# Pattern shifts as 64-bit additions on GpSimd, and two head groups' rows merged by DMA before one normalisation

## The chip, the cores and the metric

The kernel runs on one core of a Trainium2 chip. The core has five engines that run side by side: TensorE (PE in the profile, its weight loads PEld), ScalarE (ACT), VectorE (DVE), GpSimd (POOL) and SyncE (SP), which here issues the DMAs. The metric is the time of one execution on the device in microseconds (us). The kernel before took 688.67 us, the median of three runs (687.15 to 691.1).

## The reference

`x` is 2048 tokens by 512 features. Attention has 32 heads of 16 features, and a gated feed-forward part of width 1792 stands beside it; both read the same normalised input.

```
xn  = layernorm(x)
q, k, v = (xn @ wqkv), 32 heads of 16
p   = softmax(q k^T / 4)                  # 32 x 2048 x 2048 numbers
att = (p v) @ wo
g   = xn @ W_gate ;  u = xn @ W_up
glu = (max(g, 0) * u) @ W_down
out = x + att + glu
```

The softmax needs 32 x 2048 x 2048 exponentials, and most of the kernel is arranged around them.

## The kernel before

**Tiling.** Queries are cut into 4 blocks of 512 (`c4`), heads into 4 groups of 8 (`gg`), each group into two sub-groups of 4 heads (`ee`), and keys into 16 tiles of 128 (`kt`). That makes 32 blocks (c4, gg, ee) of 16 key tiles, 512 pieces in all. For one piece TensorE forms the scores of 4 heads, 128 keys by 512 queries each; something takes their exponential; and TensorE multiplies the result by the values `v_aug`. Beside the 16 values of a head `v_aug` has columns of ones, so the same product also gives the softmax's sum, in a row of its own. All these matmuls are 64 x 32 tiles of the PE array, so eight of them run side by side: two halves of the rows (`half`) by four column strips.

**Two ways to an exponential.** Most pieces go to ScalarE: two "units" each, one ACTIVATE Exp of 128 x 1024 (L1506) that reads two PSUM banks (L1504 writes them; there are two such pairs, `P_sc`) and writes one of 16 slots of `ring`. 153 pieces, called VectorE groups or quads here (`quad`, L1451), are approximated instead. VectorE adds a bias to the scores and rounds to 16-bit integers, whose bits read as bf16 give 2 to that power with a straight-line fraction (L1459, four per group, PSUM to `qd`). Two more patterns of the same 2048 numbers follow, with 31 and 81 added to every integer; the value product uses all three, which averages the error away. So a VectorE group costs TensorE three value products where a ScalarE piece costs one. `QUADS` lists how many groups each of the 32 blocks has, 359 pieces are left to ScalarE, and that makes 718 exponential instructions.

**Where the two patterns are made.** A shift is an integer addition on 128 x 2048 16-bit numbers. On GpSimd it is done as 32-bit additions of 31 x 65537 or 81 x 65537, in two pieces of 128 x 512 words (L1475, `POOL_PIECES`), with the constant broadcast from the tensor `shift` (L704). On VectorE it is one 16-bit tensor_scalar (L1479). `POOL_SHARE` and `POOL1_SHARE` say which share goes to GpSimd: all of the second patterns and 0.6 of the first. Those of the last two groups (`LASTD`) stay on VectorE.

**Normalisation** (`normalise`, L1326 on). When a block's value product is complete, VectorE copies it from PSUM to one of two `o_sb` buffers (L1338). A DMA gathers the sums (`rsum`, L1354), VectorE takes reciprocals (L1355), a DMA puts them on the rows of `rb` (L1358), VectorE spreads them over 16 rows each (STREAM_SHUFFLE, L1365), and GpSimd multiplies (L1369 for ee = 0, L1374 for ee = 1). The values of ee = 0 stand in rows 0 to 15 of each strip of 32 and those of ee = 1 in rows 16 to 31, so GpSimd adds the two products (L1377) to one `oT` tile for the output projection. This is done for 31 blocks; the last has a chain of its own (`normalise_last`).

**Order.** Nothing is ordered by the chip. `Graph.run` places every operation in time with durations written into the code (904 ns for the exponential, 601 for L1459, `POOL_NS` for a pattern and so on), some slack after DMAs (`REC_SLACK`, `MUL_SLACK`) and a priority for each engine; each engine's program is then that fixed order, with semaphore waits between engines. Background work for TensorE (projections of q, k and v, the feed-forward part, the output projection) is spread as jobs over the units. `JOB_SHIFT` and `QUAD_SHIFT` move 15 jobs by some units and 22 groups by one key tile.

Of the kernel before, what the change touches and what calls it, by code (L numbers as in the profile page):

```python
# [5 lines left out]
BF16 = mybir.dt.bfloat16  # L6
FP32 = mybir.dt.float32
I32 = mybir.dt.int32
I16 = mybir.dt.int16
U16 = mybir.dt.uint16  # L10
ACTF = mybir.ActivationFunctionType
ALU = mybir.AluOpType
# [4 lines left out]
DH = 16  # L17
# [4 lines left out]
NB = 4  # L22
NGG = 4
# [42 lines left out]
EV_DVE = ()  # L66
XN_WAIT = 0
SPREAD_NS = 660
ADD_NS = 1100
# [3 lines left out]
QUAD_SHIFT = {(4, 4): -1, (30, 1): 1, (26, 0): -1, (20, 2): -1, (30, 2): 1, (27, 0): 1, (7, 0): 1, (6, 0): -1, (4, 3): 1, (18, 2): -1, (9, 3): 1, (11, 1): -1, (11, 0): 1, (8, 1): -1, (29, 1): -1, (6, 1): 1, (30, 4): -1, (31, 3): -1, (27, 2): -1, (20, 4): -1, (21, 3): 1, (21, 0): 1}  # L73
XN_POOL = ()
XN_NS = 2080
RBZ_AT = 20
# [1 line left out]
P1_OFF = 0  # L78
# [10 lines left out]
SHIFTS = (0, 31, 81)  # L89
# [514 lines left out]
def bass_parallel_sum__mha_block__glu_gated_reglu__prompt_kernel(  # L604
# [13 lines left out]
    with ExitStack() as es:  # L618
        def sb(name, shape, dt):
            return es.enter_context(nc.sbuf_tensor(name, shape, dt))  # L620

        ident = sb("ident", [128, 128], BF16)
        ints = sb("ints", [128, 4], I32)
        pid, shift = ints[:, 0:2], ints[:, 2:4]
# [29 lines left out]
        rsum = sb("rsum", [128, 2, 16], FP32)  # L654
        rrec = sb("rrec", [128, 2, 16], FP32)
        oT1 = sb("oT1", [128, 2, 512], BF16)
# [5 lines left out]
        G = Graph()  # L662
# [11 lines left out]
        P_o = Pool("o", 2)  # L674
        P_rb = Pool("rb", 2)
        P_oT = Pool("oT", 8)
        P_o1 = Pool("o1", 2)
        P_xr = Pool("xr", 2)


# [21 lines left out]
        t_vones, t_woz, t_selp, t_shift = Tile(), Tile(), Tile(), Tile()  # L702
        for i in range(2):
            G.op("POOL", 200, lambda e, i=i: e.iota(shift[:, i:i + 1], pattern=[[0, 1]], base=SHIFTS[i + 1] * 65537, channel_multiplier=0), writes=[t_shift], prio=14, after=14)  # L704
        G.op("POOL", 300, lambda e: e.tensor_copy(identf[:], ident[:]), reads=[t_id], writes=[t_selp], prio=15, after=25)
        G.op("POOL", 100, lambda e: e.tensor_copy(selp[:], ident[:, DH - 1:128:32]), reads=[t_id], writes=[t_selp], prio=16, after=26)
        G.op("POOL", 2500, lambda e: e.memset(v_aug[:, :, :, DH:VW], 1.0), writes=[t_vones], prio=-500)
# [75 lines left out]
        def ln_block(b, pr):  # L783
# [7 lines left out]
            def inv(m, n, rd, wr):  # L791
                t_ve = Tile()
                G.op("DVE" if single else "POOL", 66 if single else 230, lambda e: e.tensor_scalar(vare[:, m:m + n], mv[:, m:m + n, 1], EPS, None, op0=ALU.add),
                     reads=[rd], writes=[t_ve], prio=pr)
                G.op("POOL", 400 + 160 * n, lambda e: e.tensor_tensor(rstd[:, m:m + n], vare[:, m:m + n], expo[:, 0:n], ALU.pow),  # L795
                     reads=[t_ve, t_expo], writes=[wr], prio=pr)
            for i in range(4):
                m = 4 * b + i
                t_st, t_mv = Tile(), Tile()
# [31 lines left out]
            for i in range(4):  # L831
# [43 lines left out]
                elif half == 1:  # L875
# [203 lines left out]
        for b in range(1, NB):  # L1079
            ln_block(b, LN_AT[b])  # L1080
            proj_k(0, b, LN_AT[b] + 1, gap=0.02)
        for kt in range(NT):
            proj_v(kt, V_AT[kt // 4] + 2 * (kt % 4), allowed=(1, 2, 3))

# [10 lines left out]
        def oT_of(t):  # L1095
            return x_sb[:, t.slot, :]
# [136 lines left out]
        busy = {int(p) for _, s, _ in plan for p in s}  # L1233


        pv_tile, last_rec, where, first_part = {}, {}, {}, {}

        def normalise_last(tp, tp_hi):

# [88 lines left out]
        def normalise(c4, gg, ee, second):  # L1328
            tp, tp_hi = pv_tile[(c4, gg, ee, second)]
            if (c4, gg, ee) == (NB - 1, NGG - 1, 1):  # L1330
                last_pv.extend(pv_tile[(c4, gg, ee, second)])
                return
            g = 2 * gg + ee
            n = c4 * 8 + g
            to = first_part.get(n)
            if to is None:
                to = Tile("o", P_o)
                G.op("DVE", 603, lambda e: e.tensor_copy(o_sb[:, to.slot, :], ps[:, BANK[tp.slot], :]), reads=[tp], writes=[to], prio=-950, name="oev%d" % n)  # L1338
                if not second:
                    first_part[n] = to  # L1340
                    return
            else:
                G.op("DVE", 603, lambda e: e.tensor_tensor(o_sb[:, to.slot, :], ps[:, BANK[tp.slot], :], o_sb[:, to.slot, :], ALU.add),
                     reads=[tp, to], joins=[to], prio=-950, name="oev%d" % n)
            if tp_hi is not tp:
                G.op("DVE", 603, lambda e: e.tensor_tensor(o_sb[:, to.slot, :], ps[:, BANK[tp_hi.slot], :], o_sb[:, to.slot, :], ALU.add),
                     reads=[tp_hi, to], joins=[to], prio=-950, name="oev%d" % n)
            pr = at_unit[place[(c4, gg, ee, NT - 1)] + 2] + 1
            ts, trr, trb = Tile("rs"), Tile("rr"), Tile("rb", P_rb, [ee])
            par = n % 2  # L1350
            if n >= 2:
                ts.r.extend(last_rec[n - 2][0].r)
                trr.r.extend(last_rec[n - 2][1].r)
            dma(lambda e: e.dma_start(rsum[:, par, :], o_sb[DH - ee:128:32, to.slot, :]), 8, reads=[to], writes=[ts], prio=pr - 50, stream=("n1", n % 4))  # L1354
            G.op("DVE", 190, lambda e: e.reciprocal(rrec[:, par, :], rsum[:, par, :]), reads=[ts], writes=[trr], prio=-940, name="rec", slack=REC_SLACK)  # L1355

            r0 = DH * ee
            dma(lambda e: e.dma_start(rb[r0:128:32, trb.slot, :], rrec[:, par, :]), 8, reads=[trr, t_rbz], writes=[trb], prio=pr - 50, stream=("n2", n % 4))  # L1358
            last_rec[n] = (ts, trr)
            if n >= len(blocks) - 3:  # L1360

                for o in ts.w + trb.w:
                    o.urgent = 1
# [3 lines left out]
            if not ee:  # L1367
                tn = t_oT[(c4, gg)] = Tile("oT", P_oT)
                G.op("POOL", 1390, lambda e: e.tensor_tensor(oT_of(tn), o_sb[:, to.slot, :], rb[:, trb.slot, :], ALU.mult),  # L1369
                     reads=[to, trb, tsp], writes=[tn], prio=pr, port=True, slack=MUL_SLACK)  # L1370
                return

            t1, tn = Tile("o1", P_o1), t_oT[(c4, gg)]
            G.op("POOL", 1390, lambda e: e.tensor_tensor(oT1[:, t1.slot, :], o_sb[:, to.slot, :], rb[:, trb.slot, :], ALU.mult),  # L1374
                 reads=[to, trb, tsp], writes=[t1], prio=pr, port=True, slack=MUL_SLACK)

            G.op("POOL", ADD_NS, lambda e: e.tensor_tensor(oT_of(tn), oT_of(tn), oT1[:, t1.slot, :], ALU.add), reads=[t1, tn], writes=[Tile()], prio=pr, port=True)  # L1377
            tn.w.append(G.ops[-1])

        pv_left, pv_ops, last_pv = {}, {}, []  # L1380
        v_flat = v_aug[:].rearrange("p kt h d -> p kt (h d)")
# [69 lines left out]
        def quad(key, u, prev):  # L1451
# [16 lines left out]
            tb, xb = made("qb")  # L1468
            nq[0] += 1
            for n, (t, x) in enumerate(((ta, xa), (tb, xb))):  # L1470
                share, off = ((POOL1_SHARE, P1_OFF), (POOL_SHARE, 0.0))[n] if nq[0] <= len(kinds) - LASTD else (0.0, 0.0)
                if int(nq[0] * share + off) > int((nq[0] - 1) * share + off):
                    m = 1024 // POOL_PIECES
                    for i in range(POOL_PIECES):
                        G.op("POOL", POOL_NS / POOL_PIECES + 60, lambda e, x=x, n=n, c=slice(i * m, i * m + m): e.tensor_tensor(  # L1475
                            x().bitcast(I32)[:, c], raw().bitcast(I32)[:, c], shift[:, n:n + 1].to_broadcast([128, m]), ALU.add),
                            reads=[ti, tq, t_shift], writes=[t] if i == 0 else [], joins=[] if i == 0 else [t], prio=u, name="p3", port=True)
                    continue
                G.op("DVE", 600, lambda e, n=n, x=x: e.tensor_scalar(x(), raw(), float(SHIFTS[n + 1]), None, op0=ALU.add),  # L1479
                     reads=[ti, tq], writes=[t], prio=u, name="d%d" % (n + 2), port=True)  # L1480
# [78 lines left out]
```

## Time and profile before

| what | before |
|---|---|
| median of three runs | 688.67 us |
| the profiled execution's span | 686.2 us |
| TensorE busy | 674.6 us, 22242 matmuls |
| ScalarE busy | 669.2 us, of it 661.4 us in 718 exponentials |
| VectorE busy | 610.8 us |
| GpSimd busy | 552.0 us, of it 485.3 us in 482 pattern pieces |
| first exponential starts, last starts | 10.4 us, 675.5 us |

The span is the profiled execution's own time, from its first instruction to its last; the page has no time around it. It is 2.5 us below the median of the runs. A row of the page's part 5 gives the line, the engine, the operation, what it writes and reads, how often it ran, then its busy time in us, the mean time of one in ns, and the engine's idle time before such instructions with what ended it. Instructions overlap at their ends, so busy time divided by the count is shorter than the mean of one.

### The profile page before, as it was taken

How to read it: one execution, taken by the hardware profiler on the slowest of the kernel's cores; microseconds unless marked ns; L12 is line 12 of the kernel's file. 1: busy time of each engine (PE TensorE's matmuls, PEld its weight loads, DVE VectorE, ACT ScalarE, POOL GpSimd, SP SyncE). 2: the span in 40 equal slices, each digit the busy share in tenths (PEclk: the TensorE clock that was granted, in tenths of full speed). 3: DMA queues.
4: the chain of work that ended last, by engine and by line, in shares of the span. 5: the costliest groups of instructions: out<-in, count | busy, mean ns of one | idle time of the engine just before them, and what ended most of it. 6: DMA issues, size and time to landing. Idle time of an engine off the chain costs nothing.

```text
span 686.2 us, 46500 instructions
## 1 busy us (share of the span) xinstructions
PE 674.6 (98%) x22242; PEld 387.1 (56%) x21226; DVE 610.8 (89%) x1059; ACT 669.2 (98%) x735; POOL 552.0 (80%) x560
## 2 busy tenths in 40 slices
PE   8999999999999999999999999999999999999997
PEld 3556655565565656665655565656455565655553
DVE  8948999999998897999999988999999888998777
ACT  7999999999999999999999999999999999999995
POOL 3522887877988989988989989899989898998780
PEclk9999999999999999999999999999999999999999
DMA  6520011132200111010100111010100121110001
GB/s 200 87 51 21 13 37 43 35 89 85 57 12 21 36 49 46 13 36 12 35 14 11 44 43 37 25 39 4 43 7 19 29 66 36 43 42 23 13 13 33
DMA packets 49561, 26.83 MB, mean 39 GB/s; under 512 B 17880, under 2 KB 49368, under 8 KB 49368
## 3 DMA queue, kind: packets, MB, share of 16 engines
q1 hardware_dynamic: 49224, 23.73, 13.3%
q8 instruction: 170, 2.79, 1.7%
q14 instruction: 23, 0.19, 0.1%
q10 hardware_dynamic: 144, 0.13, 0.1%
HBM read 18.22 MB, written 2.10 MB: 30 GB/s over the span
## 4 chain that ended last, share of the span: by engine, by line
PE 88%; ACT 8%; DVE 3%; issue 1%; DMA 0%; POOL 0%; DVEq 0%
PE ps L136 87%; ACT ring L1506 8%; DVE stats L811 1%; DVE qd L1459 0%; DMA x_sb<-in_A_x_dram 0%; DVE xn_sb L834 0%; DVE mv L813 0%; POOL rstd L795 0%; DVE xnT L879 0%; PE ps L1249 0%; DVE qT L1061 0%; DVE xn_sb L1293 0%; DVE qf L951 0%; DVE o_sb L1338 0%; DVE kT L967 0%
## 5 line engine op out<-in xcount | busy, mean ns | idle before, releaser
L1506 ACT ACTIVATE ring<-ps 128x1024 bf16<-128x1024 f32 x718 | 661.4, 1117 | 4.9 <-PE ps L136 4.1
L1475 POOL TENSOR_TENSOR qd<-qd,ints 128x512 int32<-128x512 int32 x482 | 485.3, 1040 | 94.2 <-DVE qd L1479 60.2
L136 PE MATMUL ps<-qT,kT 64*32 64x512 bf16 x8192 | 463.3, 374 | 1.8 <-ACT ring L1506 0.7
L1459 DVE TENSOR_SCALAR qd<-ps 128x512 int16<-128x512 f32 x612 | 400.8, 684 | 47.0 <-PE ps L136 42.1
L136 PE MATMUL ps<-qd,v_aug 64*32 64x512 bf16 x3672 | 297.1, 375 | 0.9 <-DVE qd L1459 0.2
L136 PE MATMUL ps<-ring,v_aug 64*32 64x512 bf16 x2872 | 251.2, 375 | 1.3 <-issue 1.0
L1439 PEld LDWEIGHTS <-kT 64*32 64x32 bf16 x8136 | 174.5, 92 | 119.7 <-issue 27.2
L1411 PEld LDWEIGHTS <-v_aug 64*32 64x32 bf16 x5584 | 135.2, 92 | 70.3 <-issue 13.3
L136 PE MATMUL ps<-xnT,wus 64*32 64x512 bf16 x1792 | 136.2, 375 | 0.0
L136 PE MATMUL ps<-xnT,wgs 64*32 64x512 bf16 x1792 | 135.6, 375 | 0.3 <-issue 0.3
L909 PEld LDWEIGHTS <-hT 64*32 64x32 bf16 x1792 | 44.4, 92 | 26.2 <-issue 4.2
L136 PE MATMUL ps<-Wd,hT 64*32 64x512 bf16 x768 | 58.2, 375 | 0.4 <-DVE qd L1459 0.4
L909 PEld LDWEIGHTS <-wgs 64*32 64x32 bf16 x1792 | 43.5, 92 | 21.8 <-issue 2.7
L909 PEld LDWEIGHTS <-wus 64*32 64x32 bf16 x1792 | 43.8, 92 | 20.1 <-issue 3.0
L1479 DVE TENSOR_SCALAR qd<-qd 128x2048 int16<-128x2048 int16 x65 | 47.9, 746 | 0.4
L1125 DVE COPY up_sb<-ps 128x512 f32<-128x512 f32 x56 | 38.5, 687 | 5.6 <-PE ps L136 5.2
L136 PE MATMUL ps<-Wk,hT 64*32 64x512 bf16 x512 | 41.7, 375 | 0.0
L136 PE MATMUL ps<-Wv,hT 64*32 64x512 bf16 x512 | 39.6, 375 | 0.3 <-issue 0.3
L1129 DVE SCALAR_TENSOR_TENSOR hT<-ps,up_sb 128x512 bf16<-128x512 f32 x56 | 38.2, 682 | 1.4 <-PE ps L136 1.4
L136 PE MATMUL ps<-Wo_p,x_sb 64*32 64x512 bf16 x480 | 37.2, 375 | 0.2
L136 PE MATMUL ps<-xnT,Wq 64*32 64x512 bf16 x480 | 35.8, 375 | 0.1
L136 PE MATMUL ps<-xnT,Wk 64*32 64x512 bf16 x480 | 35.6, 375 | 0.3 <-DVE xnT L879 0.3
(83 smaller groups left out, 307.3 us busy)
## 6 DMA issues: line engine op xcount, KB each, us to landing
wus<-in_B_W_up_dram SPq DMA_DIRECT2D x38, 128.0 KB, 2.5
wgs<-in_B_W_gate_dram SPq DMA_DIRECT2D x38, 128.0 KB, 2.4
xr_sb<-in_A_x_dram SPq DMA_DIRECT2D x16, 128.0 KB, 2.6
qT<-qf SPq DMA_DIRECT2D x120, 16.0 KB, 2.3
out_dram<-xn_sb SPq DMA_DIRECT2D x15, 128.0 KB, 1.8
x_sb<-in_A_x_dram SPq DMA_DIRECT2D x8, 128.0 KB, 2.5
Wd<-in_B_W_down_dram SPq DMA_DIRECT2D x6, 128.0 KB, 2.3
Wv<-in_A_wqkv_dram SPq DMA_DIRECT2D x1, 512.0 KB, 4.7
```

Source lines behind the costliest of these rows:

```text
L136: return e.add_instruction(mybir.InstMatmult(name=e.bass.get_next_instruction_name(), engine=mybir.EngineType.PE, ins=[e.lower_ap(x), e.lo ...
L811: G.op("DVE", 580, lambda e, m=m: e.bn_stats(stats[:, m, :], xs(m)), reads=[t_xm[m]], writes=[t_st], prio=pr, order=last_xn if m == 4 and ...
L909: e.ldweights(w()[rows, 32 * j:32 * j + 32], tile_position=(rows.start, 32 * j))
L1125: G.op("DVE", 603, lambda e: e.tensor_copy(up_sb[:, tup.slot, :], bank_of(tu)), reads=[tu], writes=[tup], prio=-590)
L1129: G.op("DVE", 603, lambda e: e.scalar_tensor_tensor(out=hT[:, th.slot, :], in0=bank_of(tg), scalar=0.0, in1=up_sb[:, tup.slot, :], op0=ALU ...
L1411: e.ldweights(vs(j), tile_position=(64 * half, 32 * j))
L1439: e.ldweights(ks(m), tile_position=(64 * half, 32 * m))
L1459: G.op("DVE", 601, lambda e, j=j, tx=tx: e.tensor_scalar(qd[:, tq.slot, 512 * j:512 * j + 512], ps[:, BANK[tx.slot], :], IBIAS[3], 0.0, op ...
L1475: G.op("POOL", POOL_NS / POOL_PIECES + 60, lambda e, x=x, n=n, c=slice(i * m, i * m + m): e.tensor_tensor(x().bitcast(I32)[:, c], raw().bi ...
L1479: G.op("DVE", 600, lambda e, n=n, x=x: e.tensor_scalar(x(), raw(), float(SHIFTS[n + 1]), None, op0=ALU.add), reads=[ti, tq], writes=[t], p ...
L1506: exp_ops[u] = G.op("ACT", 904, lambda e, tr=tr, k0=k0: e.activation(ring[:, tr.slot, :, :], ps[:, 4 * k0:4 * k0 + 2, :], ACTF.Exp, scale= ...
```

## The change

- **Patterns.** On GpSimd a pattern is one `int64_add` over 128 x 512 64-bit words (128 x 1024 32-bit words in the program) with the constant in the instruction. GpSimd makes all patterns but those of the first two groups (`FIRSTD`) and the last two (`LASTD`): 308 instructions where there were 482 pieces; VectorE makes 8 where it made 65. The operation belongs to a library that is loaded once, after the last power operation of the layernorm.
- **Normalisation.** Blocks ee = 0 and ee = 1 of a head group share it. For ee = 0 only the sums are gathered. For ee = 1 the sums are gathered too, and four DMAs of 32 KB copy rows 16 to 31 of each strip from its `o_sb` buffer into that of ee = 0. Then one reciprocal of 128 x 32, two DMAs to `rb`, one spread and one multiplication follow, the last on VectorE. The block before the last is normalised alone. So 31 reciprocals and 31 spreads become 16, and 31 multiplications and 15 additions on GpSimd become 16 multiplications on VectorE.
- **Groups.** `QUADS` has 158 groups, not 153: 354 pieces, 708 exponentials, are left to ScalarE.
- **Shifts.** `JOB_SHIFT` and `QUAD_SHIFT` are empty.

```diff
-POOL_PIECES = 2
-POOL1_SHARE = 0.6
+POOL1_SHARE = 1.0
+FIRSTD = 2
...
-JOB_SHIFT = {36: -1, 46: 6, 85: -6, 18: -2, 40: 2, 109: 4, 107: -6, 98: 4, 33: 1, 26: 6, 41: 2, 68: -1, 103: -4, 45: 1, 65: -6}
-QUAD_SHIFT = {(4, 4): -1, (30, 1): 1, (26, 0): -1, ...}
+JOB_SHIFT = {}
+QUAD_SHIFT = {}
...
-POOL_NS = 1900
-QUADS = [0, 3, 4, 5, 5, 5, 5, 5, 5, 5, 5, 5, 5, 5, 5, 5, 5, 5, 6, 5, 5, 5, 5, 5, 5, 5, 5, 5, 5, 5, 5, 5]
+POOL_NS = 1060
+LIB_NS = 7000
+LANES = 0x0001000100010001
+QUADS = [0, 3, 4, 5, 5, 6, 5, 5, 5, 5, 6, 5, 5, 5, 5, 6, 5, 5, 5, 6, 5, 5, 5, 5, 6, 5, 5, 5, 5, 6, 5, 5]
...
+        def load_library():
+            stock = [o for o in G.ops if o.eng == "POOL" and o.name == "stock"]
+            G.op("POOL", LIB_NS, lambda e: e.int64_add(word.bitcast(I64), word.bitcast(I64), 0), reads=[t_word], writes=[t_lib], prio=-790, order=stock)
...
+            if ee:
+                dma(lambda e: e.dma_start(rsum[:, par, 16:32], o_sb[DH - 1:128:32, to.slot, :]), 8, reads=[to], prio=pr - 50, stream=("n1", n % 4))
...
+                for j in range(4):
+                    rows = slice(32 * j + DH, 32 * j + 32)
+                    dma(lambda e, rows=rows: e.dma_start(o_sb[rows, toA.slot, :], o_sb[rows, to.slot, :]), 32, reads=[to], joins=[toA], prio=pr - 49, stream=("mg", j))
...
-                G.op("POOL", 1390, lambda e: e.tensor_tensor(oT_of(tn), o_sb[:, to.slot, :], rb[:, trb.slot, :], ALU.mult),
-                     reads=[to, trb, tsp], writes=[tn], prio=pr, port=True, slack=MUL_SLACK)
...
-            G.op("POOL", ADD_NS, lambda e: e.tensor_tensor(oT_of(tn), oT_of(tn), oT1[:, t1.slot, :], ALU.add), reads=[t1, tn], writes=[Tile()], prio=pr, port=True)
+            G.op("DVE", 600, lambda e: e.tensor_tensor(oT_of(tn), o_sb[:, toA.slot, :], rb[:, trb.slot, :], ALU.mult),
+                 reads=[toA, trb, tsp], writes=[tn], prio=-930, port=True, slack=MUL_SLACK, name="mul")
...
-                    for i in range(POOL_PIECES):
-                        G.op("POOL", POOL_NS / POOL_PIECES + 60, lambda e, x=x, n=n, c=slice(i * m, i * m + m): e.tensor_tensor(
-                            x().bitcast(I32)[:, c], raw().bitcast(I32)[:, c], shift[:, n:n + 1].to_broadcast([128, m]), ALU.add),
...
+                    G.op("POOL", POOL_NS, lambda e, x=x, n=n: e.int64_add(x().bitcast(I64), raw().bitcast(I64), SHIFTS[n + 1] * LANES),
+                        reads=[ti, tq, t_lib], writes=[t], prio=u, name="p3", port=True)
```

More of the change, by code (lines that the diff above doesn't have):

```diff
@@ L623, in bass_parallel_sum__mha_block__glu_gated_reglu__prompt_kernel @@
         ints = sb("ints", [128, 4], I32)
-        pid, shift = ints[:, 0:2], ints[:, 2:4]
+        pid, word = ints[:, 0:2], ints[:, 2:4]
         hmask = sb("hmask", [128, 4], FP32)
@@ L701, in bass_parallel_sum__mha_block__glu_gated_reglu__prompt_kernel @@
             t_rbz.w.append(G.ops[-1])
-        t_vones, t_woz, t_selp, t_shift = Tile(), Tile(), Tile(), Tile()
-        for i in range(2):
-            G.op("POOL", 200, lambda e, i=i: e.iota(shift[:, i:i + 1], pattern=[[0, 1]], base=SHIFTS[i + 1] * 65537, channel_multiplier=0), writes=[t_shift], prio=14, after=14)
+        t_vones, t_woz, t_selp, t_lib, t_word = Tile(), Tile(), Tile(), Tile(), Tile()
+        G.op("POOL", 100, lambda e: e.memset(word, 0), writes=[t_word], prio=-899)
         G.op("POOL", 300, lambda e: e.tensor_copy(identf[:], ident[:]), reads=[t_id], writes=[t_selp], prio=15, after=25)
@@ L1347, in normalise @@
                      reads=[tp_hi, to], joins=[to], prio=-950, name="oev%d" % n)
+            alone = (c4, gg) == (NB - 1, NGG - 1)
             pr = at_unit[place[(c4, gg, ee, NT - 1)] + 2] + 1
[L1349 to L1359, printed above, removed]
+            m = c4 * NGG + gg
+            par, r0 = m % 2, DH * ee
+            if not ee:
+                ts = Tile("rs")
+                if m >= 2:
+                    ts.r.extend(last_rec[m - 2][0].r)
+                dma(lambda e: e.dma_start(rsum[:, par, 0:16], o_sb[DH:128:32, to.slot, :]), 8, reads=[to], writes=[ts], prio=pr - 50, stream=("n1", n % 4))
+                halves[m] = to, ts, G.ops[-1]
+                if not alone:
+                    return
@@ new lines, in normalise @@
+            toA, ts, sum0 = halves[m]
+            if ee:
+                dma(lambda e: e.dma_start(rsum[:, par, 16:32], o_sb[DH - 1:128:32, to.slot, :]), 8, reads=[to], prio=pr - 50, stream=("n1", n % 4))
+                ts.w.append(G.ops[-1])
+                if m >= 2:
+                    for r in last_rec[m - 2][0].r:
+                        G.ops[-1].deps[r] = True
+                evac = [w for w in toA.w]
+                for j in range(4):
+                    rows = slice(32 * j + DH, 32 * j + 32)
+                    dma(lambda e, rows=rows: e.dma_start(o_sb[rows, toA.slot, :], o_sb[rows, to.slot, :]), 32, reads=[to], joins=[toA], prio=pr - 49, stream=("mg", j))
+                    for w in evac + [sum0]:
+                        G.ops[-1].deps[w] = True
@@ new lines, in normalise @@
+            trr, trb = Tile("rr"), Tile("rb", P_rb, [1 if alone else 0])
+            if m >= 2:
+                trr.r.extend(last_rec[m - 2][1].r)
+            w = 16 * (ee + 1)
+            G.op("DVE", 190, lambda e: e.reciprocal(rrec[:, par, 0:w], rsum[:, par, 0:w]), reads=[ts], writes=[trr], prio=-940, name="rec", slack=REC_SLACK)
+            for h in range(ee + 1):
+                dma(lambda e, h=h: e.dma_start(rb[DH * h:128:32, trb.slot, :], rrec[:, par, 16 * h:16 * h + 16]), 8, reads=[trr, t_rbz],
+                    writes=[] if h else [trb], joins=[trb] if h else [], prio=pr - 50 + 0.1 * h, stream=("n2", 2 * par + h))
+                if h:
+                    for d in G.ops[-2].deps:
+                        G.ops[-1].deps[d] = True
@@ L1360, in normalise @@
+            last_rec[m] = (ts, trr)
             if n >= len(blocks) - 3:
-                for o in ts.w + trb.w:
-                    o.urgent = 1
+                for o in ts.w + trb.w + toA.w:
+                    if o.eng == "SP":
+                        o.urgent = 1
             tsp = Tile()
@@ L1366, in normalise @@
                  reads=[trb], writes=[tsp], joins=[trb], prio=-935, name="spread", slack=REC_SLACK)
-            if not ee:
-                tn = t_oT[(c4, gg)] = Tile("oT", P_oT)
-                G.op("POOL", 1390, lambda e: e.tensor_tensor(oT_of(tn), o_sb[:, to.slot, :], rb[:, trb.slot, :], ALU.mult),
-                     reads=[to, trb, tsp], writes=[tn], prio=pr, port=True, slack=MUL_SLACK)
[L1371 to L1375, printed above, removed]
-            G.op("POOL", ADD_NS, lambda e: e.tensor_tensor(oT_of(tn), oT_of(tn), oT1[:, t1.slot, :], ALU.add), reads=[t1, tn], writes=[Tile()], prio=pr, port=True)
-            tn.w.append(G.ops[-1])
+            tn = t_oT[(c4, gg)] = Tile("oT", P_oT)
+            G.op("DVE", 600, lambda e: e.tensor_tensor(oT_of(tn), o_sb[:, toA.slot, :], rb[:, trb.slot, :], ALU.mult),
+                 reads=[toA, trb, tsp], writes=[tn], prio=-930, port=True, slack=MUL_SLACK, name="mul")
         pv_left, pv_ops, last_pv = {}, {}, []
```

18 lines of the change are left out of this document (7 added, 11 removed).

## Prediction

> **What bounds the kernel now.** I read the granted clock first (full speed in every slice of the page), then the groups of part 5, then busy time by stage, then the chain.
>
> ```profile
> L1506 ACT ACTIVATE ring<-ps 128x1024 bf16<-128x1024 f32 x718 | 661.4, 1117 | 4.9 <-PE ps L136 4.1
> L1475 POOL TENSOR_TENSOR qd<-qd,ints 128x512 int32<-128x512 int32 x482 | 485.3, 1040 | 94.2 <-DVE qd L1479 60.2
> L1459 DVE TENSOR_SCALAR qd<-ps 128x512 int16<-128x512 f32 x612 | 400.8, 684 | 47.0 <-PE ps L136 42.1
> L1479 DVE TENSOR_SCALAR qd<-qd 128x2048 int16<-128x2048 int16 x65 | 47.9, 746 | 0.4
> ```
>
> The exponentials on ScalarE run without a break: 661.4 us for 718 is 0.92 us each, and the engine was idle 4.9 us in all before them, nearly always because TensorE's scores were late. GpSimd was idle 94 us before its pieces and VectorE 47 us before its evacuations, so neither sets the pace. By stage:
>
> ```profile
> 60.00:200.00 140.00, 139.81 (x4729) 81.60 (x4496) 131.15 (x221) 140.00 (x154) 112.66 (x110) 1.00 0.17 46
> 200.00:350.00 150.00, 148.92 (x4992) 88.86 (x4795) 135.55 (x231) 149.09 (x163) 135.45 (x133) 1.00 0.11 30
> 500.00:650.00 150.00, 149.21 (x5049) 85.59 (x4732) 133.17 (x225) 149.47 (x163) 132.33 (x130) 1.00 0.12 32
> ```
>
> The columns are the stretch, its length, then busy us and instructions of PE, PEld, DVE, ACT and POOL, and the clock. ScalarE is full (fourth pair). TensorE looks full too, but its matmuls overlap, so that says little. How much room it has comes from the chain of waits, where TensorE works with nothing to wait for:
>
> ```profile
> 657.83 0.76 issue
> 658.59 7.59 PE ps L136 x266
> 666.18 0.18 issue
> 666.36 10.72 PE ps L136 x364
> ```
>
> Start, length, what, count: 266 matmuls in 7.59 us are 28.5 ns each, my price for a tile matmul. The instruction order of the built programs has 30.9 matmuls between two exponentials' scores (means from the 41st exponential on), so TensorE needs 30.9 x 28.5 = 0.88 us where ScalarE takes 0.92. **ScalarE is the bound; TensorE is 4% behind it**, and any lump in its order shows as idle ScalarE.
>
> **The change, part by part.** All sums are against the profiled span, 686.2 us, which is 2.5 us under the median of the runs; I add the difference to the median.
>
> 1. *Five more VectorE groups.* Ten exponentials go: 10 x 0.92 = -9.2 us on ScalarE, the bound. TensorE gets 5 x 24 pattern matmuls more and 10 x 4 ring matmuls fewer, 80 in all, 80 x 28.5 = 2.3 us, spread over the run: 31.3 matmuls to an exponential, 0.89 us of 0.92. Still under, by 3%. But where three successive exponentials get more matmuls than 3 x 0.92 us allow, ScalarE idles; that is 184 of 676 such stretches in the order before and 209 of 666 after, 1.14 times as many, so its 4.9 us of idle become about 5.5: +0.6. Bounds: 0 (such lumps are absorbed) to 1.5 (the lumps join).
>
> 2. *A lump at the end.* With the shifts emptied, the order of the new program has one stretch that no other has: before the 697th of 708 exponentials TensorE does 132 matmuls (output projection and held-back value products) where 40 is the most elsewhere after the start. 132 x 28.5 = 3.76 us against 0.92. ScalarE may have one exponential in hand (two score buffers), so it idles between 3.76 - 2 x 0.92 = 1.9 and 3.76 - 0.92 = 2.8 us: +2.4.
>
> 3. *The tail.* After the last exponential's scores the order has 226 matmuls, not 150; the 76 more are value products and output rows, which the last normalisation waits for. 76 x 28.5 = 2.2 us. In the trace before, the last scores start at 674.9 us and the last value product ends at 677.1; in these 2.2 us 52 matmuls are due, 1.5 us, so some 0.7 us can be filled: +1.5 (1.5 to 2.2).
>
> 4. *The pattern on GpSimd.* No run here has an `int64_add`. The nearest rows are
>
> ```profile
> L1475 POOL TENSOR_TENSOR qd<-qd,ints 128x512 int32<-128x512 int32 x482 | 485.3, 1040 | 94.2 <-DVE qd L1479 60.2 <-DVE qd L1459 22.9 <-PE ps L136 9.2
> L707 POOL MEMSET v_aug<- 128x1024 bf16 x1 | 1.0, 1012 | 0.0
> L705 POOL CAST identf<-ident 128x128 f32<-128x128 bf16 x1 | 0.3, 296 | 0.0
> L706 POOL CAST selp<-ident 128x4 f32<-128x4 bf16 x1 | 0.2, 191 | 0.0
> ```
>
> It writes 1024 words to a partition. From below: writing 1024 elements took 1.01 us. With one input: the two casts differ by 124 elements and 105 ns, 0.85 ns an element, so 191 + 1020 x 0.85 = 1.06 us. From above: as two pieces at the two-input rate, 485.3 / 482 each, 2.01 us. The instruction has one tensor input and a constant, so I take 1.06. GpSimd then works 308 x 1.06 = 326 us in place of 485 + 57 (the rows of L1369, L1374 and L1377: 20.5 + 19.2 + 17.4), and it costs nothing: it is off the path with half the span to spare. What it costs if the cover goes is rival D.
> [...]
>
> 5. *The library load.* GpSimd's last power operation ends at 26.2 us and its next need, after the change, is the third group's patterns: VectorE makes those of the first two. In the trace before GpSimd's third group starts at 58.9 us. So some 30 us of cover; a load of up to that costs nothing. Above it each us delays one group's product. I take 0.
>
> 6. *VectorE.* Busy time by rows: +20 evacuations x 0.655 (400.8 / 612) = 13.1; -57 patterns x 0.737 = -42.0; -15 spreads x 0.742 = -11.1; -15 reciprocals x 0.24 = -3.6; +16 multiplications, nearest row 0.69 (128x512 f32 from two inputs, L1343) = +11.0. Sum -32.6: 610.8 becomes 578. VectorE was not the bound, so this gives 0. The reciprocal now waits for two gathers, the multiplication for the merge. Behind them in VectorE's fixed order stand evacuations of scores, and TensorE waits for those. In the trace before, none of the 31 reciprocals and 31 spreads kept VectorE idle; the merge has the same shape as the qT copies (2.3 us to landing) and is issued with the gathers, ahead of reciprocal, second DMA and spread, so it lands first. 0; uncovered, 16 x the delay, up to 16 x 2.3 = 37 us.
>
> 7. *Buffers and queue.* An `o_sb` buffer of ee = 0 is now held for a block and its normalisation. A block lasts some 22 exponentials, 20 us; copy, gather, reciprocal, second DMA, spread and multiplication are 0.7 + 2.3 + 0.2 + 2.3 + 0.7 + 0.7 = 7 us, about 12.5 with the planned slack of 3.0 and 2.5. The other buffer serves the next block meanwhile: 0. SP issues 60 DMAs more, behind the same waits as the gathers; feed-forward weights queued behind them are asked for 38 units ahead, about 35 us: 0.
>
> Sum: -9.2 + 0.6 + 2.4 + 1.5 = **-4.7 us**. 686.2 - 4.7 = 681.5 us of span, 688.7 - 4.7 = **684.0 us** for the median, 0.7% faster. (This kernel's measurement can tell about 0.5%, 3.4 us, from no change.)
>
> **Rivals.**
>
> - *B, ScalarE alone counts.* Lump and tail fill gaps of TensorE: -9.2 us, 679.5. For it: 0.92 us each all the way and lighter neighbours (VectorE -33, GpSimd -216 us). Against: the order of the engines is fixed, so a lump of 132 is really run.
> - *C, TensorE is the bound.* If 28.5 ns is too little in the dense stretches (all of 500 to 650 us gives 29.7 ns a matmul), fewer exponentials buy nothing: +2.3 for 80 matmuls, lumps cost nothing more, 691.0. For it: 29.7 x 31.3 = 0.93 us, over ScalarE's 0.92. Against: that 29.7 is paced by ScalarE, which was idle 0.5 us of those 150.
> - *D, the addition is slow, and patterns come late.* Room for a pattern, counted in the orders from the group's last score to the pattern's first use, shrinks: the least is 80 matmuls for a first pattern (88 before), 104 for a second (164 before). Two patterns at 1.06 us save 2 x 0.95 us and the second one's room lost 60 x 28.5 = 1.7 us. So from about 1.15 us a pattern upward TensorE can start to wait, and behind it everything. At 2.01 us GpSimd is the bound outright: 58.9 + 308 x 2.01 = 678 us, then 17 us as after the last pattern piece before (669.2 to 686.2), 695 us of span, 697.5 for the median. This is slower, by 1.3%. For it: only two-input additions are in the trace, and a carry between words is more work. Against: one input, and room before was never used up (no TensorE wait on GpSimd in the table of waits).
> - *The change does not do what it says*, a pattern not in one instruction: excluded, since the built program has 308.
>
> **Chances.** Forecast 0.56, B 0.14, C 0.13, D 0.17. The forecast's own range from its bounds is -9.2 + (0 + 1.9 + 1.5) = -5.8 to -9.2 + (1.5 + 2.8 + 2.2) = -2.7 us, 682.9 to 686.0; about three quarters of it is faster by over 0.5%. Faster: 0.42 + 0.14 = 0.56; within 0.5%: 0.14 + 0.13 = 0.27; slower: 0.17. The range takes in B and C and the near half of D: 678.5 to 693.0.
>
> **What would show it.** The exponentials' row should read x708 with about 652 us; ScalarE's idle before them 7 to 9 us, with one gap of about 2.4 us some 11 us before the last exponential. From the last exponential's end to the span's end I expect about 11.3 us (9.8 before). The `int64_add` row should be x308 near 1060 ns, with no TensorE or PEld row in the waits that names GpSimd. A mean over 1150 ns with such waits is D. Idle ScalarE spread evenly, with TensorE at 29 ns or more a matmul, is C. VectorE idle before its reciprocal, spread or multiplication would overthrow step 6. The forecast fails if the lump's matmuls turn out to be waits on something else in the new order.

## The result, and the profile after

The changed kernel took 691.5 us (median of 18 runs) beside 689.79 us for the kernel before (18 runs): a ratio of 1.0031, with a 95% interval of 1.0016 to 1.0045. It is 0.3% slower where 0.7% faster was forecast. The profiled execution's span is 689.4 us, 3.2 us more than before.

First the groups of part 5, to be held against the first fence of the prediction:

```profile
L1525 ACT ACTIVATE ring<-ps 128x1024 bf16<-128x1024 f32 x708 | 651.7, 1115 | 8.2 <-PE ps L138 8.1
L1495 POOL INT64_ADD qd<-qd x308 | 317.2, 1040 | 309.5 <-DVE qd L1481 176.7
L1481 DVE TENSOR_SCALAR qd<-ps 128x512 int16<-128x512 f32 x632 | 413.3, 685 | 59.4 <-PE ps L138 53.1
```

Almost everything is as forecast: 708 exponentials of 0.92 us, a pattern of 1.04 us, ScalarE idle 8.2 us, VectorE down to 588 us and GpSimd to 330. The span does not show the gain. The table of waits names the reason, which the forecast does not have (who waited, for whom, total us, times, longest):

```profile
POOL ints L687 <- issue: 7.7, 1, 7.7
ACT xnT L866 <- PE ps L858: 7.3, 2, 6.8
DVE up_sb L1130 <- PE ps L138: 7.3, 13, 1.9
DVE ints L688 <- POOL ints L687: 7.1, 1, 7.1
...
POOL ints L886 <- issue: 6.3, 1, 6.3
```

In the fourth row VectorE's first computation behind two memsets waits 7 us for GpSimd's first behind four memsets: the iota that numbers the partitions. In the order of time, GpSimd's first instructions before (start, us, line; an idle time in brackets):

```profile
0.34 0.10 POOL L1544 MEMSET const-uint8-127<- 128x1 uint8 x1
0.84 0.14 POOL L687 IOTA ints<- 128x2 int32 x1 [0.39 <-POOLq L1544]
0.91 0.10 POOL L693 MEMSET expo<- 128x4 f32 x1
```

and after, with VectorE's beside them:

```profile
0.34 0.10 POOL L1563 MEMSET const-uint8-127<- 128x1 uint8 x1
8.10 0.13 POOL L687 IOTA ints<- 128x2 int32 x1 [7.66 <-issue]
8.19 0.09 POOL L693 MEMSET expo<- 128x4 f32 x1
```

```profile
8.26 1.16 DVE L688 TENSOR_SCALAR ints<-ints 128x2 int32<-128x2 int32 x1 [7.12 <-POOL ints L687]
9.46 0.34 DVE L691 TENSOR_SCALAR hmask<-ints 128x1 f32<-128x1 int32 x4
9.71 0.68 DVE L810 BATCH_NORM_STATS2 stats<-x_sb 128x6 f32<-128x512 bf16 x1
```

The same iota at the same line, 7.3 us later, with nothing on the page that GpSimd did in between ("issue"). Behind it in VectorE's fixed order stands the layernorm, and behind that all else: the first exponential starts at 18.8 us, not 10.4.

That is 8.4 us, 1.1 us more than the iota's delay. TensorE stood idle for 6.7 us meanwhile, and when it began again its granted clock was about half (the third number from the end; the stretch from 12 to 16 us, before and then after):

```profile
12.00:16.00 4.00, 3.38 (x71) 1.57 (x78) 3.88 (x11) 3.25 (x4) 0.65 (x1) 1.00 0.35 114
12.00:16.00 4.00, 3.43 (x44) 2.09 (x48) 3.56 (x15) 2.29 (x4) 1.63 (x4) 0.50 0.50 171
```

From 20 to 676.4 us it is 1.00 in both. That the lower clock makes the 1.1 us is not shown.

Split at the first and the last exponential, the two profiled spans differ as follows. The 0.917 us is ScalarE's mean for one exponential from 500 to 650 us before (149.47 us for 163).

| stretch | before | after | difference | forecast |
|---|---|---|---|---|
| start to first exponential | 10.4 | 18.8 | +8.4 | 0 |
| ten exponentials fewer, 0.917 us each | | | -9.2 | -9.2 |
| ScalarE late: first exponential's start to the last's end, less 0.917 us for each | 7.8 | 10.2 | +2.4 | +0.6 and +2.4 |
| last exponential's end to the end | 9.5 | 11.1 | +1.6 | +1.5 |
| span | 686.2 | 689.4 | +3.2 | -4.7 |

Without its first row the table would sum to -5.2 us.

### The profile page after: what moved, and what is told of

Its sections match the earlier page's. It is cut to its first block, busy times and chain, and to the rows that moved or that the text cites. A ratio compares the mean times of both kernels' runs of the same rounds, so it can differ in the third digit from the quotient of the medians.

```text
span 689.4 us, 46060 instructions
## 1 busy us (share of the span) xinstructions
PE 673.2 (98%) x22320; PEld 399.4 (58%) x20890; DVE 588.5 (85%) x993; ACT 659.8 (96%) x725; POOL 330.0 (48%) x340
## 4 chain that ended last, share of the span: by engine, by line
PE 82%; ACT 12%; DVE 4%; issue 2%; POOL 0%; DVEq 0%; POOLq 0%
PE ps L138 81%; ACT ring L1525 12%; DVE stats L810 1%; DVE qd L1481 1%; PE ps L1039 1%; PE ps L858 0%; DVE qd L1498 0%; DVE xn_sb L1298 0%; POOL rstd L794 0%; DVE v_aug L978 0%; DVE kT L971 0%; DVE xnT L878 0%; DVE ints L688 0%; DVE qT L1065 0%; DVE up_sb L1277 0%
## 5 line engine op out<-in xcount | busy, mean ns | idle before, releaser
L1525 ACT ACTIVATE ring<-ps 128x1024 bf16<-128x1024 f32 x708 | 651.7, 1115 | 8.2 <-PE ps L138 8.1
L1495 POOL INT64_ADD qd<-qd x308 | 317.2, 1040 | 309.5 <-DVE qd L1481 176.7
L1481 DVE TENSOR_SCALAR qd<-ps 128x512 int16<-128x512 f32 x632 | 413.3, 685 | 59.4 <-PE ps L138 53.1
L138 PE MATMUL ps<-qd,v_aug 64*32 64x512 bf16 x3792 | 301.4, 375 | 0.2
L138 PE MATMUL ps<-ring,v_aug 64*32 64x512 bf16 x2832 | 241.9, 375 | 0.6 <-issue 0.5
L1433 PEld LDWEIGHTS <-v_aug 64*32 64x32 bf16 x5252 | 128.2, 92 | 64.1 <-issue 11.2
L138 PE MATMUL ps<-xnT,wgs 64*32 64x512 bf16 x1792 | 137.5, 375 | 0.0
L138 PE MATMUL ps<-Wk,hT 64*32 64x512 bf16 x512 | 39.2, 376 | 0.0
L138 PE MATMUL ps<-xnT,Wq 64*32 64x512 bf16 x480 | 37.2, 375 | 0.0
L138 PE MATMUL ps<-Wv,xnT 64*32 64x512 bf16 x512 | 30.7, 375 | 0.3
```

Of the source, the lines that this page charges most:

```text
L138: return e.add_instruction(mybir.InstMatmult(name=e.bass.get_next_instruction_name(), engine=mybir.EngineType.PE, ins=[e.lower_ap(x), e.lo ...
L1433: e.ldweights(vs(j), tile_position=(64 * half, 32 * j))
L1481: G.op("DVE", 601, lambda e, j=j, tx=tx: e.tensor_scalar(qd[:, tq.slot, 512 * j:512 * j + 512], ps[:, BANK[tx.slot], :], IBIAS[3], 0.0, op ...
L1495: G.op("POOL", POOL_NS, lambda e, x=x, n=n: e.int64_add(x().bitcast(I64), raw().bitcast(I64), SHIFTS[n + 1] * LANES), reads=[ti, tq, t_lib ...
L1525: exp_ops[u] = G.op("ACT", 904, lambda e, tr=tr, k0=k0: e.activation(ring[:, tr.slot, :, :], ps[:, 4 * k0:4 * k0 + 2, :], ACTF.Exp, scale= ...
```

## Experiments

**Is the late start a library load, left to each execution by the one before it?** The changed kernel loads GpSimd's library for the addition once, at 34 to 41 us, as planned (6.3 us of idle time before the `int64_add` of L886, which starts at 40.72 us). My theory (L): the next execution then finds that library in place, needs the other one for its first iota, and loads it at the start, where everything waits. Two kernels test it from both sides. The first gives GpSimd a last instruction that needs the iota's library, after its last pattern.

```diff
+        pats = [o for o in G.ops if o.name == "p3"]
+        G.op("POOL", LIB_NS, lambda e: e.iota(word, pattern=[[0, 2]], base=0, channel_multiplier=1), writes=[t_word], prio=1e6, order=pats)
         for o, u in paces:
```

> The changed kernel with one more GpSimd instruction: after the last pattern an iota into a spare word, which needs the library that the first iota of the kernel needs too. Theory L: the changed kernel leaves another library in GpSimd than the one its first instructions need, so each execution begins with a load of some 7.3 us (first iota at 8.1 us, 0.84 before), and everything waits for it. Loaded back at the end, where GpSimd has had its last pattern and nobody waits for it, the load goes from the start: first iota below 1 us, first exponential back from 18.6 to some 10.3 us, span 689.4 - 8.0 = 681 us, ratio to before 0.992. Rival H: the late start comes from something else than what the execution before left behind (the first instructions, or a load that every execution makes); then the first iota stays at 8 us and the span at 689 us, or rises by what the second load costs at the end.

Measured: 683.34 us, ratio 0.9918 (0.9893 to 0.9943), span 681.0 us. GpSimd's first and last rows:

```profile
1.07 0.13 POOL L687 IOTA ints<- 128x2 int32 x1 [0.64 <-POOLq L1565]
...
```

```profile
660.81 1.04 POOL L1495 INT64_ADD qd<-qd  x1 [0.46 <-PE ps L138]
668.79 0.64 POOL L1543 IOTA ints<- 128x2 int32 x1 [6.94 <-issue]
```

The 7 us of "issue" have moved from the start to 661.9 to 668.8 us, 12 us ahead of the end, and the span is 8.4 us shorter. The other rows of the table stay as they were: the first exponential starts at 10.3 us, ScalarE is late by 10.2 us and the tail is 11.2 us. The second kernel is the kernel before with one addition as GpSimd's last instruction; the order of all other engines is the same.

```diff
+I64 = mybir.dt.int64
...
+        G.op("POOL", 7000, lambda e: e.int64_add(warm[:].bitcast(I64), warm[:].bitcast(I64), 0), reads=[t_warm], writes=[t_warm], prio=1e6, order=[o for o in G.ops if o.eng == "POOL"])
         for o, u in paces:
```

> The kernel before with one int64_add on a spare word as GpSimd's last instruction; all else, and the order of every other engine, is the same. Theory L: the next execution starts with the other library in place, the first iota comes at about 8.1 us instead of 0.84, and span and median rise by 7.5 to 8.3 us (ratio 1.011 to 1.012), although the added instruction itself stands where nobody waits for it. Rival H: no change (ratio 1.000), since nothing that stands at the start or on the path is touched.

Measured: 697.43 us, ratio 1.0116 (1.0081 to 1.0151). Its first iota:

```profile
7.96 0.13 POOL L688 IOTA ints<- 128x2 int32 x1 [7.52 <-issue]
```

One instruction at the very end, for which nobody waits, costs 1.2%, and it is paid at the start. Rival H is out: it expected the first iota to stay where it was in both. That the state was carried from one execution to the next is shown by the pair: the first iota comes at 8.10 us in the changed kernel and at 1.07 in e1_back, at 0.84 in the kernel before and at 7.96 here.

**What are ten exponentials worth (theory A against rival C)?** The kernel of the first experiment with 153 groups:

```diff
-QUADS = [0, 3, 4, 5, 5, 6, 5, 5, 5, 5, 6, 5, 5, 5, 5, 6, 5, 5, 5, 6, 5, 5, 5, 5, 6, 5, 5, 5, 5, 6, 5, 5]
+QUADS = [0, 3, 4, 5, 5, 5, 5, 5, 5, 5, 5, 5, 5, 5, 5, 5, 5, 5, 6, 5, 5, 5, 5, 5, 5, 5, 5, 5, 5, 5, 5, 5]
```

> The kernel of e1_back with the list of groups of the kernel before: 153 VectorE groups, 718 exponentials. Its order has no lump (40 matmuls at most between two exponentials after the start, as before) and 166 matmuls after the last scores, 226 in e1_back. Theory A (ScalarE is the bound, as predicted): against e1_back ten exponentials more, +9.2, no lump -2.9, tail -1.7, stalls -0.5: +4.1 us, and some 685 us of span, close to the kernel before (686.2), since the lighter VectorE and GpSimd buy nothing by themselves. Rival C (TensorE is the bound): against e1_back 80 matmuls less, -2.3 us, and lump and tail bring nothing or up to -1.7: 677 to 679 us.

Measured: 690.15 us, ratio 1.0002 (0.9979 to 1.0026), span 688.0. Against the 681.0 of its sister on the same chip that is +7.0: A's sign, but more than A's 4.1. By the rows of the table it is +9.2 for ten exponentials, -3.4 for ScalarE's lateness (6.8 us, not 10.2), as A had it, and +1.2 for the tail, which grew to 12.4 us where A had it shrink by 1.7. C, which expected 677 to 679 us, falls in this form. The ScalarE row has 8.9 us more busy time than its sister's (651.9) and less idle time (7.6 there):

```profile
L1525 ACT ACTIVATE ring<-ps 128x1024 bf16<-128x1024 f32 x718 | 660.8, 1114 | 4.4 <-PE ps L138 4.1
```

**Do lumps in TensorE's order cost what they weigh?** The kernel before with its two lists empty:

```diff
-JOB_SHIFT = {36: -1, 46: 6, 85: -6, ...}
-QUAD_SHIFT = {(4, 4): -1, (30, 1): 1, ...}
+JOB_SHIFT = {}
+QUAD_SHIFT = {}
```

> The kernel before with the two lists of shifts empty, nothing else. Its order then has three stretches of 144, 144 and 116 matmuls before one exponential where before 40 is the most, and 186 matmuls after the last scores, not 150. Theory A: each such lump idles ScalarE by its price less one or two exponentials: 144 x 28.5 = 4.1 us, 2.3 to 3.2 each, 116 x 28.5 = 3.3, 1.5 to 2.4; with the tail's +1.0: +7.1 to +9.8 us, span 693 to 696 us (ratio 1.010 to 1.014). Rival: if lumps are absorbed (TensorE gains back later, ScalarE is not really the bound), 0 to +1 us.

Measured: 697.09 us, ratio 1.012 (1.0094 to 1.0146). ScalarE's order of time has the three gaps (those in brackets over 1 us):

```profile
249.43 330.12 ACT L1506 ACTIVATE ring<-ps 128x1024 bf16<-128x1024 f32 x359 [3.10 <-PE ps L136]
...
658.17 3.77 ACT L1506 ACTIVATE ring<-ps 128x1024 bf16<-128x1024 f32 x4 [2.69 <-PE ps L136]
664.70 20.27 ACT L1506 ACTIVATE ring<-ps 128x1024 bf16<-128x1024 f32 x22 [2.76 <-PE ps L136]
```

There are three gaps for three lumps. They lasted 3.10, 2.69 and 2.76 us; worked out were 2.3 to 3.2 us for two of them and 1.5 to 2.4 for the third, so the third is longer than its price in any case. The changed kernel has its one, too:

```profile
665.34 12.94 ACT L1525 ACTIVATE ring<-ps 128x1024 bf16<-128x1024 f32 x14 [2.85 <-PE ps L138]
```

The other side is to take that lump away. One group moves from block 29 to block 18, in the kernel of the first experiment:

```diff
-QUADS = [0, 3, 4, 5, 5, 6, 5, 5, 5, 5, 6, 5, 5, 5, 5, 6, 5, 5, 5, 6, 5, 5, 5, 5, 6, 5, 5, 5, 5, 6, 5, 5]
+QUADS = [0, 3, 4, 5, 5, 6, 5, 5, 5, 5, 6, 5, 5, 5, 5, 6, 5, 5, 6, 6, 5, 5, 5, 5, 6, 5, 5, 5, 5, 5, 5, 5]
```

> e1_back with one group moved: block 29 of 0 to 31 has 5 groups, not 6, and block 18 has 6, not 5. Still 158 groups, 708 exponentials; no stretch over 40 matmuls after the start, 222 matmuls after the last scores (226 in e1_back). Theory A (a lump in TensorE's order idles ScalarE by its price less what is in hand): the 2.96 us that the 694th exponential lost go, the rest stays: span 681.0 - 3.0 - 0.1 = 678 us, ratio to before 0.988. Rival C (TensorE is the bound): the same matmuls stand elsewhere in the order and take as long: 681 us.

Measured: 680.98 us, ratio 0.9907 (0.9876 to 0.9938). The interval covers both theories, and e1_back ran on another chip. A second variant has its group moved to block 6 (5 groups there become 6):

> As f1_nolump, with the group moved from block 29 to block 6: one stretch of 52 matmuls (at the 175th exponential), 206 matmuls after the last scores. Theory A: against e1_back the lump's 2.96 us go, 52 matmuls cost 1.5 - 0.9 = 0.6 at most, 20 matmuls less in the tail are -0.6: 678.0 to 678.5 us, equal to f1_nolump within 1 us. Rival C: 681 us.

Measured: 682.9 us, ratio 0.9921 (0.9906 to 0.9937), span 682.0: not 678. So both kernels again, on one chip:

> The kernel of e1_back once more, on the chip of the next run, to weigh the lump against it. Its span was 681.2 us in the middle of four runs beside 688.1 for the kernel before: 7 us below before is expected again.

> The kernel of f1_nolump once more, on the same chip as g1_back_again. Theory A: 3.0 us below g1_back_again (the 2.96 us of the 694th exponential). Theory R: TensorE holds the same matmuls elsewhere, and ScalarE, with 3 to 4% of room between them, loses part of it again in many small stalls: 0.5 to 1.5 us below. Rival C: equal.

Measured: 683.86 us, ratio 0.9906 (0.9886 to 0.9926) with the lump, and 683.77 us, 0.9905 (0.9876 to 0.9934) without. ScalarE's last stretches, with the lump and then without:

```profile
570.92 81.72 ACT L1525 ACTIVATE ring<-ps 128x1024 bf16<-128x1024 f32 x89 [0.20 <-PE ps L138]
655.49 13.00 ACT L1525 ACTIVATE ring<-ps 128x1024 bf16<-128x1024 f32 x14 [2.85 <-PE ps L138]
```

```profile
563.79 3.77 ACT L1525 ACTIVATE ring<-ps 128x1024 bf16<-128x1024 f32 x4 [0.46 <-PE ps L138]
568.06 78.70 ACT L1525 ACTIVATE ring<-ps 128x1024 bf16<-128x1024 f32 x85 [0.49 <-PE ps L138]
647.09 24.20 ACT L1525 ACTIVATE ring<-ps 128x1024 bf16<-128x1024 f32 x26 [0.33 <-PE ps L138]
```

The gap of 2.85 us is gone, and gaps of 0.3 to 0.5 us stand in its place; others are too short to show as idle time, since one exponential begins before the last has ended (without the lump the mean of one is 1.091 us, and 708 of them are busy for 654.1 us, 0.924 us each). By the measure of the table above ScalarE is late by 8.9 us with the lump and 11.8 without. That difference is not one of the kernels, though: the first profile is of the fastest of that kernel's six executions (681.86 us), the second of one 0.8 us above its median. By the medians theory A's 3.0 us do not come; R's lower end or C's "equal" remain. I cannot tell them apart at this noise. What is shown is that a lump's gap is real where it stands, and that taking it away bought nothing that can be measured.

**Was rival D's mechanism right?** Every pattern is made twice, the second time after the first has ended; the order of the other engines is that of e1_back.

```diff
+                    G.op("POOL", 0.0, lambda e, x=x, n=n: e.int64_add(x().bitcast(I64), raw().bitcast(I64), SHIFTS[n + 1] * LANES), reads=[ti, tq, t_lib], writes=[t], prio=u, lat=0.0)
                     G.op("POOL", POOL_NS, lambda e, x=x, n=n: e.int64_add(x().bitcast(I64), raw().bitcast(I64), SHIFTS[n + 1] * LANES),
```

> e1_back with every pattern made twice, the second time after the first has finished, into the same place; the order of all other engines is unchanged. A pattern then takes 2.1 to 2.2 us, about what the two pieces of the kernel before took. Rival D's mechanism, as predicted: GpSimd is busy 308 x 2.15 = 660 us and becomes the bound, TensorE waits for patterns (a row in the table of waits, PE or PEld behind GpSimd), and the span is 58 + 660 + 17 = 735 us at the most, 695 to 735 us. Theory S (there is slack enough in the order for late patterns): under 690 us.

Measured: 803.61 us, ratio 1.1675 (1.1639 to 1.171), span 799.4. The rows of the waits and of GpSimd:

```profile
PE ps L138 <- POOL qd L1496: 88.2, 95, 3.3
```

```profile
L1495 POOL INT64_ADD qd<-qd x308 | 323.4, 1050 | 77.8 <-DVE qd L1481 56.1 <-PE ps L138 21.3
L1496 POOL INT64_ADD qd<-qd x308 | 322.8, 1048 | 29.8 <-POOL qd L1495 0.2 <-DVE qd L1481 0.2
```

The sign and the wait are D's, but the time is well over what I gave as the most. GpSimd is busy 646 us of 799 and idle 108 between patterns: it is not simply the bound. A reading that fits: each late pattern stops TensorE, which delays the scores of the next group, which GpSimd then waits for. The chain that ended last bears it out in so far as it changes sides, 51% of the span through GpSimd and 36% through TensorE. By that reading lateness runs in a loop in this fixed order, and the sum of the slower engine's work is only a lower end: 646 us of patterns went with 799 us of span here.

**What does each part buy alone?** First the patterns alone: e3_back_153 with the normalisation of the kernel before (L1326 to L1378 of the code before).

> The patterns alone: e3_back_153 (int64_add, the library loaded back at the end, 153 groups, no shifts) with the normalisation of the kernel before, two multiplications and an addition on GpSimd for each head group. Order: no lump, 122 matmuls after the last scores (166 in e3_back_153), 200 of 676 dense stretches (177). Theory A (merging the normalisation is off the path; only the order counts): 688.0 - 44 x 28.5 ns = -1.3, +0.6: 687 us, within 0.3% of e3_back_153. Rival M (the merge itself gains or costs): off that by more than 2 us, upward if the 15 spreads and reciprocals taken from VectorE were worth something (22 us of VectorE's time come back), downward if the merge's DMAs and waits cost.

Measured: 1145.75 us, ratio 1.6655 (1.6627 to 1.6683). Neither theory was near. GpSimd's order of time shows it:

```profile
84.29 1.25 POOL L1377 TENSOR_TENSOR x_sb<-o_sb,rb 128x512 bf16<-128x512 f32 x1 [7.14 <-issue]
91.43 2.05 POOL L1481 INT64_ADD qd<-qd  x2 [5.88 <-issue]
95.72 1.04 POOL L1481 INT64_ADD qd<-qd  x1 [2.24 <-DVE qd L1467]
104.09 1.25 POOL L1382 TENSOR_TENSOR oT<-o_sb,rb 128x512 bf16<-128x512 f32 x1 [7.33 <-issue]
111.28 1.03 POOL L1481 INT64_ADD qd<-qd  x1 [5.94 <-issue]
```

I take every change between the addition and a tensor_tensor or iota for a load: GpSimd sits idle 5.7 to 6.3 us before the addition and 6.7 to 7.8 us before the other. There are 82 such changes in the trace, with 535 us of idle time before them. TensorE's granted clock was 0.814 here in the mean, 1.000 in the kernel before; what part of the lost time is due to it is not separated. So the merged normalisation is no small saving beside the patterns: taking GpSimd's multiplications away is what makes the patterns possible (1145.75 us with them, 690.15 without, e3_back_153). I had weighed the two parts one by one, and missed that.

Then the merged normalisation alone: after's normalisation with the 32-bit pieces, 153 groups and empty lists.

```diff
-POOL1_SHARE = 1.0
-FIRSTD = 2
+POOL_PIECES = 2
+POOL1_SHARE = 0.6
...
-                    G.op("POOL", POOL_NS, lambda e, x=x, n=n: e.int64_add(x().bitcast(I64), raw().bitcast(I64), SHIFTS[n + 1] * LANES),
+                        G.op("POOL", POOL_NS / POOL_PIECES + 60, lambda e, x=x, n=n, c=slice(i * m, i * m + m): e.tensor_tensor(
```

> The merged normalisation alone: 153 groups, no shifts, patterns as the kernel before makes them (32-bit pieces on GpSimd, 0.6 of the first ones), so one library. To be held against e5_before_noshift (695.2 us of span beside 688.1 for before), which differs by the normalisation alone. Its order has stretches of 120, 96 and 56 matmuls (144, 144, 116 there) and 194 matmuls after the last scores (186). Theory A, by those: lumps 6.4 us there against (3.4 - 1.4) + (2.7 - 1.4) + (1.6 - 1.4) = 3.5 here, tail +0.2: some 3 us below e5_before_noshift, 691 to 693 us. Rival M (the merge's DMAs and waits in VectorE's order cost): above 695.

Measured: 700.86 us, ratio 1.0153 (1.0133 to 1.0174), span 699.4: above e5_before_noshift's 1.012, not 3 us below. From the 41st exponential on the three that were latest came 3.0, 2.3 and 1.1 us late, where the lumps had been priced at 2.0, 1.3 and 0.2. What I missed more is the tail: 14.7 us after the last exponential, 10.7 there, because the order leaves a last group's scores behind the last exponential, and their evacuation, patterns and products follow one another. My count of matmuls in the tail cannot see such a chain. That the merge's own DMAs cost is not shown: VectorE's waits have no row for them.

**How far can the groups go?** The kernel f1_nolump with one group more in blocks 3, 8, 13, 21 and 27, 163 in all.

> f1_nolump with 163 groups (one more in blocks 3, 8, 13, 21 and 27): 698 exponentials, 31.95 matmuls between two, 0.911 us of 0.917. Its order has nine stretches of 60 to 120 matmuls where f1_nolump has none over 40. Theory A: ten exponentials less, -9.2; nine lumps, 732 matmuls x 28.5 ns less 1.4 us each, +8.5; 206 matmuls after the last scores, not 222, -0.5: within 1.5 us of f1_nolump, so the way ends here, since TensorE is now as full as ScalarE. If lumps are absorbed, 5 to 9 us below f1_nolump; if TensorE was the bound all along, 2 us above it.

Measured: 691.71 us, ratio 1.002 (1.0002 to 1.0039), 8 us above 158 groups. ScalarE has 698 exponentials and is idle 21.5 us before them:

```profile
L1525 ACT ACTIVATE ring<-ps 128x1024 bf16<-128x1024 f32 x698 | 645.2, 1085 | 21.5 <-PE ps L138 20.3
```

It is worse than any theory had it, and the idle time is spent waiting for TensorE. At 158 groups TensorE was 3% behind ScalarE on paper; at 163, 1%, and the nine long stretches of its order are no longer made up for.

## Why the prediction was wrong

- **Step 5 failed, the library load.** I counted the one load that the diff writes down and put it at nothing, since it had cover. That one load did have it (6.3 us of idle GpSimd at 34 to 41 us, with the next need at 65). But the kernel has two libraries now: it ends in the one and begins in the other, and it loaded at its start too (7.66 us of idle GpSimd before the first iota, 0.64 in e1_back, which ends in the one with which it begins). In the traces of both programs a record named MODIFY_POOL_CONFIG stands ahead of the first iota (at 0.74 us before, the iota at 0.84; at 0.81 us after, the iota at 8.10). Before, the iota's idle time is 0.4 us, which the pair of kernels puts down to the library that was there already; I read the price of the row and not its condition. After, the iota comes 7.3 us later and the first exponential 8.4 us later; with the load moved to the end this is gone, and the span is 8.4 us shorter (e1_back, 681.0 us). The traces give two prices for a load: 5.7 to 6.3 us of idle time ahead of an `int64_add`, 6.7 to 7.8 us ahead of an iota or a tensor_tensor (f2_patterns_only).
- **Step 1 held in its main term.** Ten exponentials came to 9.2 us. The small lateness did not grow by 0.6 us, though: without the one long gap ScalarE was late by 7.3 us, 7.8 before.
- **Step 2 held in place and size** (2.4 forecast with 2.8 as the most, 2.85 measured), but not as a separable price: the kernel without the lump is no faster. The idea behind it, that TensorE has 3% to spare and only lumps matter, was too kind to TensorE, as g4_163 shows. The 28.5 ns a matmul came from one stretch of the chain; the last line of the same fence has 364 in 10.72 us, 29.5 ns, and by that 31.3 matmuls take 0.92 us and the room is gone. Unhindered, ScalarE is also a little faster than 0.92 us: more than half of its exponentials start no more than 0.904 us after the one before, in both kernels, so it is held up by more than its idle time shows. Both engines are near their limit. That ScalarE's work still counts is shown by e3_back_153, and that the room ends soon by g4_163.
- **Step 3 held in its number** (+1.5, measured +1.6), with some luck: the same way of counting matmuls behind the last scores missed the tail in e3_back_153 (1.7 us shorter expected, 1.2 longer measured) and in g3_merge_only.
- **Step 4 held.** 1.06 us by two cast rows, 1.04 measured; by the two-input rate of the kernel before (1.01 us a piece, 2.01 for a pattern) it would have been about twice that. That a carry between words is more work, which I set down for rival D, was not shown.
- **Steps 6 and 7 held.** There was no idle time of VectorE before reciprocal, spread or multiplication, and the multiplication took 716 ns. The merge's DMAs, 32 KB each and not 16 as the qT copies with which I compared them, landed in 2.5 us. VectorE's rows changed by -31.6 us in sum (-32.6 forecast), but its busy time by -22.3 (588 us, 578 forecast): rows overlap at their ends, so their sum is not the engine's busy time.
- **The rivals.** The result, 691.5 us, fell where rival C stood (691.0), but by luck: C's mechanism was not what made it. D's wait is real with a pattern of 2.1 us (f3_twice) and costs more than I had it; at 1.04 us it did not occur. The rival that I lacked was "the change puts a load at the start".

The version that beats both kernels is the changed one with the iota's library loaded back at the end: 0.9918 and 0.9906 of before in two comparisons, against the 0.993 that I had forecast for the change itself.

## What to carry to other kernels

Price what an instruction needs in place (here a library of GpSimd) at every point where it may be missing, the kernel's first instruction included: here an execution started with the library that the one before had left (first iota at 0.84 us in the kernel before, at 7.96 in e2_before_lib). If two are needed, end in the one with which you begin, where the engine has nothing to do; here that was worth 8.4 us of span (e1_back). And before you weigh the parts of a change one by one, ask whether one part only makes another possible.

## What the runs showed of the hardware

- GpSimd's loaded library was kept from one execution to the next: the same first iota came at 0.84 us or at 7.96 us, depending on one instruction at the end of the program (before and e2_before_lib), and at 8.10 or 1.07 us in the other pair (the changed kernel and e1_back).
- `int64_add` on 128 x 512 64-bit words took 1040 ns (the changed kernel, 308 of them), half of the two 32-bit pieces with a broadcast second input (2 x 1.01 us, the kernel before) that make the same pattern.
- What I take for a library load on GpSimd stood in the profile's rows as idle time alone, mostly put down to "issue" and at times to another engine: 5.7 to 6.3 us before an `int64_add`, 6.7 to 7.8 us before a tensor_tensor or an iota (f2_patterns_only, 82 changes).
- After TensorE had stood idle for 6.7 us at the start, its granted clock was 0.50 from 12 to 16 us, and 1.00 again from 20 to 676.4 us (the changed kernel; 1.00 in these stretches before).
